# Threshold attention with a feed-forward on one core: inverted sums sent through DRAM, values a step later, and other orders of the steps

## The chip, the cores and the metric

The kernel runs on one core of a Trainium2 chip. The core has TensorE (matrix products into PSUM), VectorE, ScalarE and GpSimd for elementwise work, SyncE (SP) that only starts transfers here, and 16 DMA engines that carry what SP, ScalarE and GpSimd start. The metric is the device time of one execution in microseconds; the kernel before has a median of 528.99 us over three runs (527.98 to 530.42).

## The reference

Attention over 8 batches, 8 heads, 576 positions and 64 features, which keeps only scores close to their row's maximum, and then two dense layers over the 4608 x 512 result:

```python
scores = scale * np.matmul(q, k.transpose(0, 1, 3, 2))
thresh = np.max(scores, axis=-1, keepdims=True) - tau
scores = np.where(scores >= thresh, scores, -1000000000.0)
attn = np.exp(scores - np.max(scores, axis=-1, keepdims=True))
attn = attn / (np.sum(attn, axis=-1, keepdims=True) + 1e-09)
x = np.matmul(attn, v)             # then (batch, position, head and feature)
h = x @ w_in                       # 512 -> 2048
out = np.maximum(0.01 * h, h) @ w_out   # 2048 -> 512
```

## The kernel before

**Tiles.** Two heads make a pair; there are 32 pairs, and two pairs make a *couple*, so 16 couples, two to a batch. The 1152 query rows of a couple and head slot are cut into nine *steps* of 128 rows: steps 0 to 3 belong to the first pair, 4 to 7 to the second, step 8 takes the last 64 rows of both. In each step the two heads of the pair are worked one beside the other ("first" and "second").

**One step.** `s_mm` (L146) makes the scores of both heads from queries and keys split into a high and a low float16 part (three products). VectorE's `s_max` instruction (L182) scales them, writes them to `sn` and gives the negated row maximum; GpSimd makes a threshold `nth` from it (L187). Then a head goes one of two ways. Either ScalarE takes one exponential (L192), and a step later VectorE masks it and adds up the row (L215, in `s_mask`); or the head is *direct*: ScalarE makes two passes (L198, L202), the second of which gives the row's sum, and VectorE does nothing more. The weights `W` of both heads are turned by a DMA transpose that SP starts (L221) into `wT`.

**A couple's sums and values.** After the ninth mask the 18 sums of each of 128 partitions are inverted: `sums_0` adds a small number on GpSimd, `sums_1` inverts on VectorE and makes the high float16 part on GpSimd, `sums_2` makes the low part on VectorE. `sums_3` turns both parts by one product (L247) and ScalarE takes the result to `row`. `sums_4` spreads the rows over 64 partitions each by five or six products with a selecting matrix (L264); ScalarE takes the result to `rc` (L269). `values` (L272) multiplies `wT` by V on TensorE (20 products), and VectorE multiplies by `rc` on its way to `xT` (L290). In PSUM, the turns of queries and keys (`prep`, L123), the turned sums, the spread and the values all use the one pair of banks "A"; scores have two pairs and the dense layers two single banks "u".

**The dense layers.** When a batch's values are there (couple 2, 4, ..., step 6), `push_main` and `push_tail` put its work on a list of *units*: four products of 512 columns each into a bank "u" (L302, then ScalarE's L306), or four products of the second layer (L317). The units are handed out over the following 18 steps, in shares set by the tuple `share`; `ahead_of` says how many of a step's units come before its second head.

**The order.** All instructions are in program order on their engines; the loop at the end writes that order. For each step it takes a string of parts ("scores", "values", "first", "units", "turn_qk", "spread", "evict", "second", "more", "mask", "soon") and calls them in turn. "evict" and "soon" run ScalarE's and VectorE's deferred evictions. The couple's values come in steps 3 and 5 of the next couple, after the spreads in steps 2 and 4. Loads of q and k and the outputs go over SP's queue, V and the dense weights over GpSimd's.

Of the kernel before, what the change touches and what calls it, by code (L numbers as in the profile page):

```python
# [9 lines left out]
FP32 = mybir.dt.float32  # L10
# [6 lines left out]
def kernel(  # L17
# [24 lines left out]
    sb = ctx.enter_context(tc.tile_pool(name="sb", bufs=1))  # L42
    ps = ctx.enter_context(tc.tile_pool(name="ps", bufs=1, space=bass.MemoryType.PSUM))
# [68 lines left out]
    due = []  # L112

# [9 lines left out]
    def prep(p, i, tag="A", bufs=1):  # L123


        t = nat[p]
        pt = pair_of_banks(tag, bufs).rearrange("p a b -> p (a b)")
        for c in range(4 + i):

            nc.tensor.matmul(  # L130
                out=pt[0:128, ds(c * 128, 128)],
                lhsT=t[0:128, 4 * i + c, :, :].rearrange("p h d -> p (h d)"),
                rhs=I32[:, :],
                is_transpose=True, skip_group_check=True,
            )
# [3 lines left out]
        due.append(lambda: nc.scalar.activation(out=hi[:, :], in_=pt[:, 0:N], func=AF.Copy, bias=0.0, scale=QS))  # L139
        soon.append(lambda: nc.vector.scalar_tensor_tensor(  # L140
            out=lo[:, :], in0=pt[:, 0:N], scalar=QS, in1=hi[:, :],
            op0=OP.mult, op1=OP.subtract,
        ))
        qk.setdefault(p, {})[i] = (hi, lo)

    def s_mm(c, t):  # L146


        out = [ps.tile([128, 2, 512], FP32, tag="s", bufs=2, name="s") for _ in range(2)]
        if t < 8:  # L150
            srcs = [(2 * c + t // 4, 0, ds(t % 4 * 128, 128), ds(0, 128))]
        else:
            srcs = [(2 * c + e, 1, ds(576, 64), ds(64 * e, 64)) for e in range(2)]
        for half in range(2):
            for ti, (a, b) in enumerate(((0, 0), (1, 0), (0, 1))):
                for p, i, cols, po in srcs:
                    for h in range(2):
                        r = ds(h * 64, 64)
                        nc.tensor.matmul(  # L159
                            out=out[h][po, half, 0:288], lhsT=qk[p][i][a][r, cols],  # L160
                            rhs=qk[p][1][b][r, ds(half * 288, 288)],
                            start=(ti == 0), stop=(ti == 2), skip_group_check=True,
                        )
        sc[(c, t)] = out

    live, dens = {}, {}

    def s_max(c, t, h, direct):
# [3 lines left out]
        if t == 0 and h == 0:  # L172
            dens[c] = sb.tile([128, 18], FP32, tag="den", bufs=2, name="den")
        if h == 0:
# [20 lines left out]
        else:  # L195
# [8 lines left out]
                accum_out=dens[c][:, 2 * t + h:2 * t + h + 1],  # L204
            )

    def s_mask(c, t):
# [5 lines left out]
        for h in range(2):  # L213
            if h not in masked:
# [3 lines left out]
                    accum_out=dens[c][:, 2 * t + h:2 * t + h + 1],  # L218
                )
        q0 = 512 if t == 8 else t * 128 + (t // 4) * 128  # L220
# [4 lines left out]
    def sums_0(c):  # L225

# [6 lines left out]
    def sums_1(c):  # L233
        d1, rr = inv[c]
        nc.vector.reciprocal(out=rr[:, :], in_=d1[:, :])
        nc.gpsimd.tensor_scalar(out=r2[:, 0, 0:18], in0=rr[:, :], scalar1=1.0 / RS, scalar2=0.0,
                                op0=OP.mult, op1=OP.add)

    def sums_2(c):
        d1, rr = inv[c]  # L240
        nc.vector.scalar_tensor_tensor(out=r2[:, 1, 0:18], in0=rr[:, :], scalar=1.0 / RS, in1=r2[:, 0, 0:18],
                                       op0=OP.mult, op1=OP.subtract)

    def sums_3(c):

# [6 lines left out]

    def sums_4(c, e):

        row = rows[c]
# [12 lines left out]
        rc = sb.tile([128, 576], FP32, tag="rc", bufs=2, name="rc")  # L268
        due.append(lambda: nc.scalar.activation(out=rc[:, :], in_=t[:, 0:576], func=AF.Copy, bias=0.0, scale=1.0))  # L269
        rcs[e] = rc  # L270

    def values(c, e):  # L272
# [12 lines left out]
        rc = rcs.pop(e)  # L285
# [3 lines left out]
        def mul():  # L289
            nc.vector.tensor_tensor(  # L290
# [45 lines left out]
    def push_main(b):  # L336

# [42 lines left out]
    with tc.manual_schedule():  # L380
# [15 lines left out]
        for p in range(1, 3):  # L396
# [12 lines left out]
        before = "scores turn_qk evict first second mask soon"  # L409
        orders = {  # L410
            0: "scores turn_qk evict units first second more mask soon",
            1: "scores invert first units rest more second mask soon",
            3: "scores values first units second more mask soon",
            5: "scores first values units second more mask soon",
            6: "scores first turn_qk evict units more second mask soon",
            8: "scores first units turn_qk evict more second mask soon",
        }
        credit = 0.0
        w_at = [1 + i for i in range(32)]
        prev = None  # L420
        for c in range(NC + 1):
            last = c == NC
            for t in range(NT):
                step = c * NT + t
                if c > 1 and c % 2 == 0 and t == 6:

                    if c % 4 == 2 and c > 2:
                        push_tail(c // 2 - 3, 1)
# [5 lines left out]
                nxt = {6: (2 * c + 2, 0), 7: (2 * c + 2, 1), 8: (2 * c + 3, 0), 0: (2 * c + 1, 1)}  # L434
                if c == 0:
                    nxt[0], nxt[1] = (1, 0), (1, 1)
                pi = nxt.get(t)
                if pi is not None and pi[0] >= NP:
                    pi = None

                ahead = [share[i % NT] for i in range(step, (c // 2 * 2 + (0 if c % 2 == 0 and t < 6 else 2)) * NT + 6)]
                credit = min(credit, 1.0) + (len(units) - credit) * share[t] / sum(ahead)
                n = min(int(credit + 0.01), len(units))
                credit -= n
                n1 = min(n, (n + ahead_of[t]) // 2)
                direct = tau_f <= 16.0 and (
                    t not in (0, 1, 3) if c < 3 else t in (2, 5, 7, 8) or not any(u[0] for u in units[:n]))
                direct0 = tau_f <= 16.0 and c < 3 and t in (0, 3, 5)

                if c == 0 and t < 2 or c < 2 and t == 6:  # L450
                    order = before
                else:
                    order = orders.get(t, plain)
                    if c == 1 and t == 0:
                        order = "scores first turn_qk evict second mask soon"
                for part in order.split():
                    if part == "scores" and not last:
                        s_mm(c, t)
                    elif part == "values" and c > 0:
                        values(c - 1, t // 2 - 1)  # L460
                    elif part == "first" and not last:
                        s_max(c, t, 0, direct0)
                    elif part == "second" and not last:
                        s_max(c, t, 1, direct)
                    elif part == "invert" and c > 0:
                        sums_1(c - 1)
                    elif part == "rest" and c > 0:
                        sums_2(c - 1)
                    elif part == "units":
                        work(n1)  # L470
                    elif part == "more":
                        if c > 0 and t == 1:
                            work(n - n1 - 1)
                            sums_3(c - 1)
                            work(1 if n > n1 else 0)
                        else:
                            work(n - n1)
                    elif part == "turn_qk" and pi is not None:
                        prep(*pi)
                    elif part == "spread" and c > 0 and t in (2, 4):  # L480
                        sums_4(c - 1, t // 2 - 1)
                    elif part == "evict":
                        run(take(due))
                    elif part == "mask":
                        if prev is not None:
                            s_mask(*prev)
                        prev = None if last else (c, t)
                    elif part == "soon":
                        run(take(soon))
                if c > 0 and t == 0:  # L490
                    sums_0(c - 1)
                if c == 0 and 0 < t < 6:
                    load_v(0, t - 1)
                if c % 2 == 0 and c > 0 and t >= 4 and c // 2 < B:
                    load_v(c // 2, t - 4)
                for i in range(32):
                    if w_at[i] == step:
                        load_w(i)
                if t < 4 and 2 * c + 3 < NP:
                    load_qk(2 * c + 3, t // 2, t % 2)  # L500
                elif 4 <= t < 8 and 2 * c + 4 < NP:
                    load_qk(2 * c + 4, t // 2 - 2, t % 2)
# [36 lines left out]
```

## Time and profile before

| | |
|---|---|
| Runs (us) | 528.99, 530.42, 527.98 |
| Profiled execution | 528.58 us, its span 526.8 us |
| TensorE, VectorE, ScalarE, GpSimd busy | 94%, 79%, 84%, 35% |
| Mean granted TensorE clock | 0.969 |
| DMA | 80.5 MB, mean 153 GB/s |
| Chain that ended last | TensorE 83%, ScalarE 7%, VectorE 5% |

How to read it: busy time is what an engine's instructions took, matmuls overlap, and their ends are modelled. "[1.06 <-ACT hi L139]" behind a line says that the engine stood idle for 1.06 us before it and that ScalarE's instruction of line 139 ended the wait. PEclk is the granted clock in tenths. In the table of stretches the figure in brackets is the number of instructions. A DMA's landing is the time from its issue to its completion.

### The profile page before, as it was taken

How to read it: one execution, taken by the hardware profiler on the slowest of the kernel's cores; microseconds unless marked ns; L12 is line 12 of the kernel's file. 1: busy time of each engine (PE TensorE's matmuls, PEld its weight loads, DVE VectorE, ACT ScalarE, POOL GpSimd, SP SyncE). 2: the span in 40 equal slices, each digit the busy share in tenths (PEclk: the TensorE clock that was granted, in tenths of full speed). 3: DMA queues.
4: the chain of work that ended last, by engine and by line, in shares of the span. 5: the costliest groups of instructions: out<-in, count | busy, mean ns of one | idle time of the engine just before them, and what ended most of it. 6: DMA issues, size and time to landing. Idle time of an engine off the chain costs nothing.

```text
span 526.8 us, 12333 instructions
## 1 busy us (share of the span) xinstructions
PE 494.7 (94%) x4384; PEld 272.9 (52%) x4384; DVE 414.7 (79%) x1076; ACT 444.0 (84%) x795; POOL 186.4 (35%) x430
## 2 busy tenths in 40 slices
PE   5577787999999999999999999999999999999996
PEld 3344444555555566555555566555555565545444
DVE  5878887998899888998899888998899888982000
ACT  3896979989999899989898999989898999983622
POOL 0754446543443234323443234323433244321000
PEclk9786969999999999999999999999999999999999
DMA  6999999998997899887999689887998799853011
GB/s 154 137 164 184 205 186 198 206 183 175 164 186 145 152 173 168 167 142 165 183 170 142 150 176 188 146 138 156 189 164 152 147 169 154 116 85 93 40 41 60
DMA packets 266813, 80.50 MB, mean 153 GB/s; under 512 B 251904, under 2 KB 264192, under 8 KB 266752
## 3 DMA queue, kind: packets, MB, share of 16 engines
q1 hardware_dynamic: 249136, 70.68, 75.0%
q0 software_dynamic: 17536, 8.92, 14.8%
q8 instruction: 34, 0.56, 0.5%
q14 instruction: 27, 0.22, 0.1%
q10 hardware_dynamic: 80, 0.13, 0.1%
HBM read 36.70 MB, written 9.44 MB: 88 GB/s over the span
## 4 chain that ended last, share of the span: by engine, by line
PE 83%; ACT 7%; DVE 5%; issue 2%; DMA 2%; POOL 0%; SPq 0%; DVEq 0%; ACTq 0%; POOLq 0%
PE u L317 24%; PE u L302 22%; PE s L159 21%; PE A L280 8%; PE A L130 6%; DVE sn L182 3%; ACT W L202 2%; ACT far L198 2%; ACT e L192 2%; PE A L264 1%; DMA nat<-in_q_dram 1%; DVE W L215 1%; DMA nat<-in_k_dram 1%; ACT hi L139 1%; ACT gM L306 0%
## 5 line engine op out<-in xcount | busy, mean ns | idle before, releaser
L182 DVE TENSOR_SCALAR_CACHE_REDUCE sn<-s 128x576 f32<-128x576 f32 x288 | 207.6, 754 | 41.9 <-PE s L159 40.2
L187 POOL TENSOR_SCALAR nth<-nmx 128x1 f32<-128x1 f32 x288 | 125.6, 436 | 242.2 <-DVE sn L182 219.1
L192 ACT ACTIVATE e<-sn,nmx 128x576 f16<-128x576 f32 x181 | 137.6, 770 | 17.6 <-DVE sn L182 16.4
L215 DVE SCALAR_TENSOR_TENSOR W<-sn,nth,e 128x576 f16<-128x576 f32 x181 | 144.3, 814 | 0.0
L302 PE MATMUL u<-xT,win 128*128 128x512 f16 x512 | 122.7, 380 | 0.4 <-ACT gM L306 0.4
L317 PE MATMUL u<-wout,gM 128*128 128x512 f16 x512 | 122.1, 380 | 0.0
L159 PEld LDWEIGHTS <-hi 64*128 64x128 f16 (+1 forms) x1280 | 65.9, 99 | 70.4 <-issue 53.4
L159 PE MATMUL s<-hi,hi 64*128 64x288 f16 x512 | 87.6, 300 | 11.4 <-DVE sn L182 9.7
L159 PE MATMUL s<-hi,lo 64*128 64x288 f16 (+1 forms) x640 | 93.1, 294 | 0.0
L159 PE MATMUL s<-lo,hi 64*128 64x288 f16 (+1 forms) x640 | 92.8, 293 | 0.0
L198 ACT ACTIVATE far<-sn,nth 128x576 f32<-128x576 f32 x107 | 82.5, 771 | 8.2 <-POOL nth L187 6.3
L302 PEld LDWEIGHTS <-win 128*128 128x128 f16 x768 | 61.2, 98 | 52.5 <-issue 8.4
L202 ACT ACTIVATE W<-far,ntau 128x576 f16<-128x576 f32 x107 | 83.0, 775 | 3.5
L306 ACT ACTIVATE gM<-u 128x512 f16<-128x512 f32 x128 | 71.5, 590 | 6.8 <-PE u L302 6.8
L317 PEld LDWEIGHTS <-gM 128*128 128x128 f16 x512 | 46.5, 98 | 52.6 <-issue 7.9
L140 DVE SCALAR_TENSOR_TENSOR lo<-A,hi 128x512 f16<-128x512 f32 (+1 forms) x63 | 47.6, 755 | 17.0 <-ACT hi L139 16.6
L130 PE MATMUL A<-I,nat 128*128 128x128 f32 x283 | 45.9, 291 | 10.4 <-DVE lo L140 5.1
L139 ACT ACTIVATE hi<-A 128x512 f16<-128x512 f32 (+1 forms) x63 | 40.0, 636 | 10.1 <-PE A L130 10.1
L280 PE MATMUL A<-wT,V 128*64 128x288 f16 x640 | 48.0, 298 | 0.0
L130 PEld LDWEIGHTS A<-I,nat 128*128 128x128 f32 x283 | 32.1, 145 | 26.0 <-DVE lo L140 13.8
L280 PEld LDWEIGHTS <-V 128*64 128x64 f16 x640 | 35.1, 113 | 11.7 <-issue 8.0
L328 ACT ACTIVATE osb<-u 128x512 f32<-128x512 f32 x35 | 20.6, 590 | 23.7 <-PE u L317 23.7
(44 smaller groups left out, 302.8 us busy)
## 6 DMA issues: line engine op xcount, KB each, us to landing
nat<-in_q_dram SPq DMA_DIRECT2D x32, 256.0 KB, 3.6
nat<-in_k_dram SPq DMA_DIRECT2D x32, 256.0 KB, 3.8
out_dram<-osb SPq DMA_DIRECT2D x16, 512.0 KB, 3.6
wT<-W SPq DMA_TRANSPOSE x144, 4.1
V<-in_v_dram POOLq DMA_DIRECT2D x8, 256.0 KB, 5.7
win<-in_moe_w_in_dram POOLq DMA_DIRECT2D x16, 128.0 KB, 5.2
V<-in_v_dram POOLq DMA_DIRECT2D x16, 128.0 KB, 4.9
wout<-in_moe_w_out_dram POOLq DMA_DIRECT2D x16, 128.0 KB, 4.7
```

The source lines that it names most:

```text
L130: nc.tensor.matmul(out=pt[0:128, ds(c * 128, 128)], lhsT=t[0:128, 4 * i + c, :, :].rearrange("p h d -> p (h d)"), rhs=I32[:, :], is_transp ...
L159: nc.tensor.matmul(out=out[h][po, half, 0:288], lhsT=qk[p][i][a][r, cols], rhs=qk[p][1][b][r, ds(half * 288, 288)], start=(ti == 0), stop= ...
L182: nc.vector.tensor_scalar(out=sn[:, h, :].rearrange("p (a b) -> p a b", a=2), in0=s_[:, :, 0:288], scalar1=-BS, scalar2=None, op0=OP.mult, ...
L187: nc.gpsimd.tensor_scalar(out=nth[:, h:h + 1], in0=nmx[:, h:h + 1], scalar1=1.0, scalar2=tau_f, op0=OP.mult, op1=OP.add,)
L192: nc.scalar.activation(out=e[:, h, :], in_=sn[:, h, :], func=AF.Exp, bias=nmx[:, h:h + 1], scale=-1.0,)
L198: nc.scalar.activation(out=far[:, :], in_=sn[:, h, :], func=AF.Prelu, bias=nth[:, h:h + 1], scale=-1.0, alpha=BIG,)
L202: nc.scalar.activation(out=w[:, ds(h * 576, 576)], in_=far[:, :], func=AF.Exp, bias=ntau[:, 0:1], scale=1.0, accum_out=dens[c][:, 2 * t + ...
L215: nc.vector.scalar_tensor_tensor(out=w[:, ds(h * 576, 576)], in0=sn[:, h, :], scalar=nth[:, h:h + 1], in1=e[:, h, :], op0=OP.is_le, op1=OP ...
L280: nc.tensor.matmul(out=t[ds(h * 64, 64), half, 0:288], lhsT=vb[:, g, h, kb, :], rhs=wT[:, 4 * h + kb, ds(e * 576 + half * 288, 288)], star ...
L302: nc.tensor.matmul(out=t[:, ts(j, N)], lhsT=w_in16[:, gi, ts(j0 + j, 128)], rhs=xs[gi], start=(gi == 0), stop=(gi == NG - 1), skip_group_c ...
L306: nc.scalar.activation(out=g_out, in_=t[:, 0:nj * N].rearrange("p (j n) -> p j n", j=nj), func=AF.Prelu, bias=0.0, scale=1.0, alpha=0.01)
L317: nc.tensor.matmul(out=t[:, :], lhsT=g_in(j), rhs=w_out16[:, j, :], start=(j == 0), stop=(j == NJ - 1), skip_group_check=True,)
```

## The change

For couples 3 to 14 (`by_dma`) the sums' spread no longer uses products. The inverted sums are turned in float32 by one product of 18 columns of weights, ScalarE takes the 18 x 128 result to `row32`, GpSimd stores it to a scratch tensor in DRAM (`sums_d`, in step 1) and reads it back with four loads that each repeat one row of 640 numbers over 64 partitions (`sums_b`, in step 2). The columns of the sums are laid out so that a row of the turned sums is one head's rows in order. Couples 0 to 2 and 15 keep the old way.

The first values of a couple come in step 4 instead of 3 from couple 3 on; the second stay in step 5, in some couples behind units. The strings of parts are written anew in single letters for five classes of couples (0, 1, 2, odd and even from 3 on). The sets of direct heads are given by class (`d0` for the first head, `d1` for the second, with `d1n` for those which are never made direct for lack of first-layer units); over the whole kernel 116 heads are direct instead of 107 (8, 7, 8 instead of 9, 9, 9 in couples 0 to 2). `share` has 18 entries, `up` takes the place of `ahead_of`. Loads are placed by a table, at the same steps as before.

```diff
+def by_dma(c):
+    return 3 <= c < 15
+
+def col(c, t, h):
+    if not by_dma(c):
+        return 2 * t + h
+    return 9 * h + (t if t < 4 else 4 if t == 8 else t + 1)
...
-                accum_out=dens[c][:, 2 * t + h:2 * t + h + 1],
+                accum_out=dens[c][:, col(c, t, h):col(c, t, h) + 1],
...
 def sums_1(c):
     nc.vector.reciprocal(out=rr[:, :], in_=d1[:, :])
+    if by_dma(c):
+        return
...
 def sums_3(c):
+    if by_dma(c):
+        d1, rr = inv[c]
+        t = pair_of_banks().rearrange("p a b -> p (a b)")
+        nc.tensor.matmul(out=t[0:18, 0:128], lhsT=rr[:, :], rhs=I32[:, :], is_transpose=True,
+                         skip_group_check=True)
+        row = sb.tile([18, 128], FP32, tag="row32", bufs=2, name="row32")
+        due.append(lambda: (nc.scalar.activation(out=row[:, :], in_=t[0:18, 0:128], func=AF.Copy, bias=0.0, scale=1.0), was.add(("row", c))))
+        rows[c] = row
+        return
...
+def sums_d(c):
+    d = dr.tile([18, 128], FP32, tag="dr", bufs=2, name="dr")
+    nc.gpsimd.dma_start(out=d[:, :], in_=rows[c][:, :])
+    rows[c] = d
+
+def sums_b(c):
+    d = rows[c]
+    for e in range(2):
+        rc = sb.tile([128, 640], FP32, tag="rc", bufs=2, name="rc")
+        src = d.rearrange("(h i) q -> h (i q)", h=2)[:, ds(512 * e, 640)]
+        for h in range(2):
+            nc.gpsimd.dma_start(out=rc[ds(64 * h, 64), :], in_=src[h:h + 1, :].to_broadcast([64, 640]))
+        rcs[e] = rc[:, ds(64 * e, 576)]
...
-share = (20, 21, 23, 13, 20, 13, 26, 29, 26)
-ahead_of = (3, 3, 1, 3, -1, 1, 1, 1, -1)
-plain = "scores first units turn_qk evict spread evict second more mask soon"
+share = (23, 21, 23, 16, 20, 13, 26, 29, 32, 23, 27, 23, 16, 20, 10, 29, 29, 32)
+d0 = [[0, 1, 3, 5], [0, 3, 5], [0, 2, 3], [], []]
+d1 = [[3, 4, 5, 7], [3, 6, 7, 8], [3, 4, 5, 7, 8], [2, 3, 4, 6, 8], [0, 2, 3, 4, 5, 8]]
+d1n = [[0, 6], [3], [3], [0, 2, 3], [2, 3, 4]]
```

The order of the parts for odd couples from 3 on, one string for each step (S scores, 0 and 1 the heads, P a turn of q or k, h evictions, U, u and w units, r inversion, T turn of the sums, D store, R loads, Q old spread, V values, M masks, L deferred work of VectorE, d the sums' first instruction):

```
'S Pd h U w 0 h 1 u M d L', 'r S U 0 x T u h D 1 w M L', 'S w 0 U Q0 h 1 u R M L',
'S 0 u U w 1 M L', 'S V0 0 w U Q1 h 1 u M L', 'S U 0 V1 1 u M L', ...
```

More of the change, by code (lines that the diff above doesn't have):

```diff
@@ L225, in sums_0 @@
     def sums_0(c):
+        assert ("mask", c, 8) in was
+        was.add(("d", c))
         d1 = sb.tile([128, 18], FP32, tag="d1", bufs=1, name="d1")
@@ L336, in push_main @@
     def push_main(b):
+        assert all(("x", b, g) in was for g in range(NG))
         xs = [xTs[(b, g)][:, ds(g % 2 * 64, 512)] for g in range(NG)]
@@ L404 @@
         run(take(soon))
-        share = (20, 21, 23, 13, 20, 13, 26, 29, 26)
-        ahead_of = (3, 3, 1, 3, -1, 1, 1, 1, -1)
-        plain = "scores first units turn_qk evict spread evict second more mask soon"
[L409 to L417, printed above, removed]
@@ new lines, with at @@
+        credit = 0.0
+        plan = {}
+        def at(step, f):
+            plan.setdefault(step, []).append(f)
+        for b in range(B):
+            for i, x in enumerate([[1, 2, 3, 4, 5], [22, 23, 24, 25, 26]][b] if b < 2 else range(18 * b + 4, 18 * b + 9)):
+                at(x, lambda b=b, i=i: load_v(b, i))
+        for i, x in enumerate([1, 2, 3, 4, 5, 6, 7, 8, 9, 10, 11, 12, 13, 14, 15, 16, 17, 18, 19, 20, 21, 22, 23, 24, 25, 26, 27, 28, 29, 30, 31, 32]):
+            at(x, lambda i=i: load_w(i))
@@ L420 @@
+        for p in range(3, NP):
+            for x in range(4):
+                at((p - 3) // 2 * 9 + (p - 3) % 2 * 4 + x + 0, lambda p=p, x=x: load_qk(p, x // 2, x % 2))
+        for x in sorted(s_ for s_ in plan if s_ < 0):
+            for f in plan[x]:
+                f()
         prev = None
@@ L433 @@
                         push_tail(c // 2 - 2, 1)
[L434 to L455, printed above, removed]
@@ L456, with target @@
-                for part in order.split():
-                    if part == "scores" and not last:
-                        s_mm(c, t)
[L459 to L463, printed above, removed]
+                def target(x):
+                    return x * NT + (6 if x == 2 else 6)
+                nx = c // 2 * 2
@@ new lines, with count @@
+                if step >= target(nx) or c < 2 and 0:
+                    nx += 2
+                def count():
+                    global_ = sum(share[i % 18] for i in range(step, max(target(nx), step + 1)))
+                    return (len(units) - credit) * share[ph] / global_
+                n = None
+                for o in orders[cl][t].split():
+                    if o == "G":
+                        if c > 1 and c % 2 == 0:
+                            push()
+                            nx = c // 2 * 2 + 2
+                        continue
+                    if n is None:
+                        credit = min(credit, 1.0) + count()
+                        n = min(int(credit + 0.01), len(units))
+                        credit -= n
+                        k1 = min(n, max(0, (n + up[cl][t]) // 2))
+                        heads = [u[0] for u in units[:n]]
+                    if o == "S" and not last:
+                        s_mm(c, t)
+                    elif o[0] == "V" and c > 0:
+                        values(c - 1, int(o[1]))
+                    elif o == "0" and not last:
+                        s_max(c, t, 0, tau_f <= 16.0 and (t in d0[cl]))
+                    elif o == "1" and not last:
+                        direct = tau_f <= 16.0 and (t in d1[cl] or c > 2 and t not in d1n[cl] and not any(heads))
@@ L483 @@
                         run(take(due))
-                    elif part == "mask":
+                    elif o[0] == "Q" and c > 0 and not by_dma(c - 1):
+                        sums_4(c - 1, int(o[1]))
+                    elif o == "M":
                         if prev is not None:
                             s_mask(*prev)
-                        prev = None if last else (c, t)
-                    elif part == "soon":
+                            prev = None
+                        if not last:
+                            prev = (c, t)
+                    elif o == "L":
@@ L489 @@
                         run(take(soon))
[L490 to L502, printed above, removed]
+                for f in plan.get(step, ()):
+                    f()
```

91 lines of the change are left out of this document (63 added, 28 removed).

## The prediction

> **What bounds the kernel now.** I read the share of each engine in 40 slices first, then the same by stretches of time, then TensorE's timeline over one couple in the middle.
>
> ```profile
> PE   5577787999999999999999999999999999999996
> DVE  5878887998899888998899888998899888982000
> ACT  3896979989999899989898999989898999983622
> ...
> PEclk9786969999999999999999999999999999999999
> ```
>
> ```profile
> core 0: us, PE busy (x) PEld busy (x) DVE busy (x) ACT busy (x) POOL busy (x), PEclk, DMA share, GB/s
> ...
> 26.00:40.00 14.00, 9.79 (x89) 5.91 (x85) 10.84 (x28) 13.61 (x26) 7.35 (x16) 0.86 1.42 165
> ...
> 53.00:66.00 13.00, 9.11 (x97) 5.90 (x97) 11.10 (x27) 12.60 (x23) 6.11 (x14) 0.92 1.17 205
> ...
> 79.00:92.00 13.00, 10.35 (x109) 6.34 (x108) 9.57 (x24) 12.69 (x24) 8.11 (x17) 1.00 1.29 199
> ...
> 316.00:369.00 53.00, 53.00 (x488) 29.35 (x487) 47.59 (x126) 48.99 (x89) 18.39 (x43) 1.00 0.95 157
> ```
>
> Two regimes. From about 92 us to the end TensorE is never idle (53.00 of 53 us), ScalarE is at 92% and VectorE at 90%: there a microsecond of TensorE work is a microsecond of time. Before 92 us there are no units yet; TensorE idles 27 us, and where two keys and queries are turned (the three stretches above) ScalarE is full, at 97%. The timeline of all engines shows what that costs: VectorE stands still until ScalarE, behind its double passes, has evicted `hi`.
>
> ```profile
> 58.27 0.69 DVE L140 SCALAR_TENSOR_TENSOR lo<-A,hi 128x512 f16<-128x512 f32 x1 [1.06 <-ACT hi L139]
> ...
> 86.37 0.69 DVE L140 SCALAR_TENSOR_TENSOR lo<-A,hi 128x512 f16<-128x512 f32 x1 [1.80 <-ACT hi L139]
> ```
>
> **Term 1: the spread's products go (12 couples).** TensorE's timeline in couple 8, start and length:
>
> ```profile
> 245.50 0.22 PE L247 MATMUL A<-I,r 128*128 128x128 f16 x1
> 245.65 0.30 PE L159 MATMUL s<-hi,hi 64*128 64x288 f16 x2
> ...
> 247.37 0.42 PE L264 MATMUL A<-row,sel 128*128 128x128 f16 x5
> 247.62 1.03 PE L317 MATMUL u<-wout,gM 128*128 128x512 f16 x4
> ...
> 252.58 0.43 PE L264 MATMUL A<-row,sel 128*128 128x64 f16 x6
> 252.84 1.89 PE L317 MATMUL u<-wout,gM 128*128 128x512 f16 x8
> ```
>
> What counts is from one start to the next: 0.25 us for the first five, 0.26 us for the six, so 0.51 us a couple. All twelve couples lie in the full regime: 12 x 0.51 = 6.1 us off the path. The turn of the sums (L247, 0.15 us start to start) is replaced by a turn in float32. The rows have float32 turns of 128 columns (L130), four of them in 0.50 us at 237.34, so 0.12 us each; the mean duration of one, if nothing overlapped, is 0.29. Bounds: -0.4 to +1.7 us over twelve; I take 0, since in this regime they overlap. ScalarE loses two evictions of 0.63 us a couple and keeps a row of about 0.28; VectorE loses 0.17 and GpSimd 0.22: none is on the path there, so 0.
>
> **Term 2: the way of the sums through DRAM.** New, per couple, on GpSimd: one store of 9 KB and four loads of 164 KB. The transfers issued by GpSimd after 100 us are the nearest rows:
>
> ```profile
> V<-in_v_dram POOLq DMA_DIRECT2D x12, 128.0 KB, 4.4
> ...
> V<-in_v_dram POOLq DMA_DIRECT2D x12, 32.0 KB, 3.4
> ```
>
> Call the store's landing d and a load's b. I lay the changed order over the measured lengths (scores 0.84 us, a unit of four products 0.87, values 1.35), with zero at the start of step 1 of a couple. Scores, two units, the turn: 2.73. ScalarE's row is out at about 3.5; the store is issued there, lands at 3.5 + d. GpSimd then stands in front of the first load until d is over, and issues a load each 0.65 us (issues of V last 0.64 to 0.92). Both loads of the first half land at 4.15 + d + b. Step 4 begins at 7.87; VectorE reaches the product with the sums 3.04 us later (248.58 to 251.62 in the old couple), at 10.9. If the sums are late VectorE waits, which is free until the second values need the pair of banks: they are due at 12.6, so the product must start by 11.8. The margin is d + b = 7.65 us (in couple 4, whose step 3 has one unit, 7.2). The rows: 3.4 + 4.4 = 7.8, a stall of about 0.15 us a couple. The lowest landings of V in this regime (2.8 and 2.8) give none; 4.1 (a store of 128 KB) and 6.0 (the slowest V) give 2.5 us a couple, 29 us in all. The loads here have 64 rows in one piece each, V four pieces a row with a change of type, so I put b a little under its row; with scatter I charge 1.5 us in all.
>
> The Trainium skill, DMA: Bandwidth & Descriptors, section "Anatomy of one DMA", gives about 2.0 us plus bytes over 436 GB/s for a transfer that GpSimd issues; an estimate by it is 2.0 + 2.4 = 4.4 us for d + b, no stall, and a sum 1.5 us lower. The 32 KB of V that take 3.4 us under this kernel's traffic stand against the page, so the sum goes by the rows.
>
> What is queued behind: on GpSimd the thresholds (L187) of step 1's second head wait for the store, those of step 3 for the four loads, until about 3.5 + 3.4 + 4 x 0.65 = 9.5. ScalarE's direct pass of step 3 needs them and starts near 10 instead of 8.2 to 9.5. ScalarE has the slack to take this back in steps 4 and 5, but in couples 4, 8 and 12 it is still about 1 us late at the evictions of step 6, where the next unit then waits up to 0.5 us: I charge 0.7 us in all, bounds 0 and 6 (0.5 in each couple). The traffic grows by 0.66 MB per 29 us, 22 GB/s on 157; stretches before 92 us ran at 205, and TensorE waited for `wT` 1.3 us in the whole run, so 0. SP's queue keeps its order.
>
> **Term 3: other heads go direct.** A direct head costs ScalarE two passes, start to start 1.56 us against 0.69, and spares VectorE a mask of 0.81 (0.88 with its read). Couples 0 to 2 have 8, 7, 8 instead of 9 each. In the full stretches, two direct heads fewer each stand ahead of the late `hi`: 1.74 us less on ScalarE, 1.6 more on VectorE. At 79 to 92 VectorE has room (9.57 + 1.6 of 11.3): about 1.5 us won of the wait of 1.80. At 26 to 40 and 53 to 66 VectorE becomes equally full: about 1.0 and 0.7. Sum 3.2; I take 2.7 since masks also come into the loop between scores and minima. Bounds: 5.2 won (3 x 1.74) to 3.5 lost (four masks all exposed). In couples 3 to 15, 13 more heads are direct: 13 x 0.87 = 11 us on ScalarE against 12 x 2 x 0.63 = 15 taken away, so it stays below TensorE; VectorE loses 13 x 0.88. Cost 0 while TensorE covers it.
>
> **Moved steps.** Values and their product come a step later: nobody waits for them before the units of the next pair. At the very end eight products of old outputs (1.7 us) stand between the last values and the first new unit before, four (0.87) after; VectorE's product of 0.75 us just fits into them. The shares move units between steps, not their number. 0.
>
> **Sum.** The profiled execution took 528.58 us, 1.8 more than its span of 526.8, and 0.4 less than the median 528.99. 528.58 - 6.1 - 2.7 + 1.5 + 0.7 = 522.0; I give 522.0 for the median too.
>
> **Rivals.**
> A: the sums are late for good. Speaks for it: rows at 7.8 against a margin of 7.65, and V landings up to 6.0. Against: the waits of V and the weights in the full regime are nowhere in the list of waits. Each us over the margin costs 12. At d + b = 9.2, 1.55 us over: 528.58 - 8.8 + 18.6 + 0.7 = 539. It decides at 8.3 (no gain left); slower by 0.5% from 8.5. The Trainium skill, SBUF — State Buffer, box "The DVE blocks DMA trap (SWDGE)", would feed it: GpSimd's descriptors wait while VectorE holds the shared port. The rows bear out a hold for thresholds (0.70 us beside a mask, 0.19 alone), but issues of V never stretched past 0.92.
> B: the start doesn't move, VectorE taking ScalarE's place as its bound: 528.58 - 6.1 + 2.2 = 524.7. For it: two stretches come out equally full.
> C: ScalarE takes over in the full regime, since the waits on thresholds fall on an engine at 92%: term 2's 6 us and the start's 2.7 leave 528.58 - 6.1 - 2.7 + 1.5 + 6 = 527.3.
> D: nothing is late: 522.0 - 2.2, and the start's whole 5.2: 517.3.
>
> **How the numbers follow.** Forecast (520 to 524) 0.33; B 0.16; D 0.15; C 0.13; A 0.23. The range from 517 to 532 leaves out the far half of A and a third of D, 0.16 together. About 0.5% (2.6 us) is what a measurement of this kernel tells from no change. Faster by more: forecast, B, D and a few of C, 0.66. Same: most of C and the near part of A, 0.15. Slower: the rest of A, 0.19.
>
> **What would show it.** Right: TensorE full from about 89 us on, two couples in 58.0 us instead of 59.0 (178.98 to 238.00 in the chain), hardly any wait of VectorE's product on the loads, store and four loads landing within 7.7 us in sum of d and b, `lo` waiting less for `hi` before 92 us. Wrong: TensorE waiting for VectorE's product at the second values once a couple; units waiting for ScalarE's `gM`; or VectorE full at the start with the same 92 us.

## The result, and the profile after

The changed kernel takes 535.3 us (median of 6 runs, 531.91 to 537.37), the kernel before 528.14 us beside it: a ratio of 1.0115 (95%: 1.009 to 1.0139; the ratio is taken over the runs and is not the quotient of the two medians). It is slower, and outside the predicted range of 517 to 532. The profiled execution took 536.01 us with a span of 534.2, against 528.58 and 526.8 before: 7.4 us more span.

The busy share in 40 slices, from the page of the changed kernel:

```profile
PE   5677779999799999989899999999999999999996
...
DVE  5888989988698887978598888888898868972000
ACT  3886889988799989988699889988899988984622
...
PEclk9776879999999999999899999999999999999999
```

TensorE's row of 9s, unbroken before from the eighth slice on, now has gaps in slices 11, 18 and 20. In the last of them (254 to 267 us) VectorE falls to 5, ScalarE to 6 and the granted clock to 8 tenths. The same by stretches of time, first the changed kernel and then the one before (columns as before):

```profile
core 0: us, PE busy (x) PEld busy (x) DVE busy (x) ACT busy (x) POOL busy (x), PEclk, DMA share, GB/s
...
26.00:40.00 14.00, 10.44 (x87) 6.11 (x82) 12.01 (x32) 11.90 (x21) 6.87 (x16) 0.74 1.38 215
53.00:66.00 13.00, 9.13 (x96) 5.93 (x93) 12.53 (x33) 10.97 (x19) 6.06 (x13) 0.91 1.25 182
79.00:92.00 13.00, 11.57 (x116) 6.93 (x115) 11.58 (x30) 12.41 (x23) 8.60 (x19) 1.00 1.23 157
211.00:264.00 53.00, 48.80 (x414) 25.93 (x412) 41.28 (x109) 44.38 (x82) 19.30 (x48) 0.98 0.94 172
316.00:369.00 53.00, 52.09 (x506) 29.87 (x504) 44.74 (x115) 49.87 (x91) 21.28 (x51) 1.00 1.06 180
```

```profile
211.00:264.00 53.00, 53.00 (x468) 28.23 (x467) 47.08 (x123) 48.38 (x88) 18.33 (x44) 1.00 0.88 164
```

From 211 to 264 us TensorE, full before, is now busy for 48.80 of 53 us. What it waits for stands in the list of TensorE's waits of the changed kernel (line and what it waited for: us in total, times, longest):

```profile
PE A L336 <- DVE xT L349: 7.7, 5, 2.5
...
PE A L132 <- DVE xT L349: 3.7, 4, 1.3
```

The values (L336) and the turns of q and k (L132) wait for VectorE's product `xT`; two of the four turns (1.8 us) lie ahead of couple 3. In the kernel before no values wait for it, and two turns ahead of couple 3 do, for 1.0 us. VectorE's own list says why the product is late:

```profile
DVE xT L349 <- DMA rc<-dr: 19.9, 14, 3.6
DVE lo L144 <- ACT hi L141: 11.6, 16, 1.9
```

The product stands 14 times, 19.9 us in all, before loads of the sums. (The second line is for later: VectorE's wait for `hi` was 17.6 us before.) The chain of the changed kernel from 249 to 266 us shows the worst case, couple 8 (start, length, what):

```profile
248.58 0.58 ACT osb L387
249.16 0.16 ACT row L279
249.32 0.28 issue
249.60 3.88 DMA dr<-row
253.48 0.28 issue
253.76 0.44 POOL rc L304
254.20 0.13 issue
254.33 6.56 DMA rc<-dr
...
261.01 0.77 DVE xT L349
261.78 0.04 issue
261.82 2.61 PE A L336 x20
```

No engine bounds this stretch: the chain runs from ScalarE's row through the store (3.88 us), GpSimd's second load (6.56 us) and the product to the second values. Over the whole run the transfers carry 16% of the chain and TensorE 54%, where TensorE carried 83% before.

Lengths of couples, from one first minimum (L199, L182 before) to the next, give the account. A couple is named here by its own steps; the sums and values that are worked in them are those of the couple before it, so the way through DRAM is walked in couples 4 to 15.

| | before | after | difference |
|---|---|---|---|
| couples 0 to 2 (start of couple 3) | 94.78 | 93.40 | -1.38 |
| couple 3 | 28.22 | 29.44 | +1.22 |
| couples 4 to 14 | 324.07 | 332.27 | +8.20 |
| couple 15 to the end of the span | 79.7 | 79.1 | -0.6 |

Couple 3 has one unit of 0.87 us more, which is missing at the end; most of these two differences is that shift. In couples 4 to 14 TensorE was never idle; now it is idle for 11.0 us, of which 9.65 are waits for a late `xT` (7.77 at the second values, 1.88 at turns behind it in couples 4 and 7). Where nothing is late, odd couples take 28.98 us instead of 29.46, and even ones from 6 on 29.46 or 29.47 instead of 29.49 to 29.56: the two together 58.45 (couples 9 and 10), where 58.0 was forecast and 59.0 was the time before.

### The profile page after: what moved, and what is told of

Same layout as the page of the kernel before. It is cut to its first block, busy times and chain, and to the rows that moved or that the text cites. A ratio compares the mean times of both kernels' runs of the same rounds, so it can differ in the third digit from the quotient of the medians.

```text
span 534.2 us, 12130 instructions
## 1 busy us (share of the span) xinstructions
PE 492.0 (92%) x4252; PEld 269.7 (50%) x4252; DVE 405.8 (76%) x1046; ACT 439.5 (82%) x789; POOL 202.1 (38%) x478
## 4 chain that ended last, share of the span: by engine, by line
PE 54%; DMA 16%; ACT 14%; DVE 7%; issue 5%; POOL 2%; DVEq 0%; SPq 0%; POOLq 0%; ACTq 0%
PE u L376 18%; PE u L361 13%; PE s L165 12%; DMA rc<-dr 9%; PE A L336 5%; ACT e L209 5%; DMA dr<-row 5%; PE A L132 5%; DVE sn L199 4%; ACT gM L365 3%; ACT far L215 2%; ACT W L219 2%; DVE W L232 2%; DVE xT L349 1%; POOL rc L304 1%
## 5 line engine op out<-in xcount | busy, mean ns | idle before, releaser
L199 DVE TENSOR_SCALAR_CACHE_REDUCE sn<-s 128x576 f32<-128x576 f32 x288 | 206.5, 754 | 41.9 <-PE s L165 41.1
L204 POOL TENSOR_SCALAR nth<-nmx 128x1 f32<-128x1 f32 x288 | 111.3, 387 | 191.7 <-DVE sn L199 177.0
L209 ACT ACTIVATE e<-sn,nmx 128x576 f16<-128x576 f32 x172 | 129.5, 766 | 20.0 <-DVE sn L199 19.2
L232 DVE SCALAR_TENSOR_TENSOR W<-sn,nth,e 128x576 f16<-128x576 f32 x172 | 137.7, 815 | 0.6 <-POOL nth L204 0.6
L215 ACT ACTIVATE far<-sn,nth 128x576 f32<-128x576 f32 x116 | 89.3, 770 | 22.7 <-POOL nth L204 21.9
L219 ACT ACTIVATE W<-far,ntau 128x576 f16<-128x576 f32 x116 | 89.9, 775 | 3.8
L365 ACT ACTIVATE gM<-u 128x512 f16<-128x512 f32 x128 | 73.0, 589 | 7.1 <-PE u L361 5.9
L132 PE MATMUL A<-I,nat 128*128 128x128 f32 x283 | 45.9, 292 | 11.8 <-DMA nat<-in_q_dram 4.5
L336 PE MATMUL A<-wT,V 128*64 128x288 f16 x640 | 48.9, 303 | 8.3 <-DVE xT L349 7.7
L349 DVE TENSOR_TENSOR xT<-A,rc 128x576 f16<-128x576 f32 x32 | 24.2, 756 | 31.7 <-DMA rc<-dr 19.9
L336 PEld LDWEIGHTS <-V 128*64 128x64 f16 x640 | 37.6, 115 | 18.7 <-issue 15.9
L132 PEld LDWEIGHTS A<-I,nat 128*128 128x128 f32 x283 | 32.9, 146 | 26.9 <-DVE lo L144 8.7
```

Source lines behind the costliest of these rows:

```text
L132: nc.tensor.matmul(out=pt[0:128, ds(c * 128, 128)], lhsT=t[0:128, 4 * i + c, :, :].rearrange("p h d -> p (h d)"), rhs=I32[:, :], is_transp ...
L199: nc.vector.tensor_scalar(out=sn[:, h, :].rearrange("p (a b) -> p a b", a=2), in0=s_[:, :, 0:288], scalar1=-BS, scalar2=None, op0=OP.mult, ...
L204: nc.gpsimd.tensor_scalar(out=nth[:, h:h + 1], in0=nmx[:, h:h + 1], scalar1=1.0, scalar2=tau_f, op0=OP.mult, op1=OP.add,)
L209: nc.scalar.activation(out=e[:, h, :], in_=sn[:, h, :], func=AF.Exp, bias=nmx[:, h:h + 1], scale=-1.0,)
L215: nc.scalar.activation(out=far[:, :], in_=sn[:, h, :], func=AF.Prelu, bias=nth[:, h:h + 1], scale=-1.0, alpha=BIG,)
L219: nc.scalar.activation(out=w[:, ds(h * 576, 576)], in_=far[:, :], func=AF.Exp, bias=ntau[:, 0:1], scale=1.0, accum_out=dens[c][:, col(c, t ...
```

## The experiments

The theory after the result was rival A: the sums come too late. Against it stood that GpSimd, standing before its transfers, delays thresholds and so ScalarE (rival C), that the additional traffic as such does it, or that the new orders are worse by themselves.

### 1. The loads don't wait for the store (e2_free_loads)

```diff
-        src = d.rearrange("(h i) q -> h (i q)", h=2)[:, ds(512 * e, 640)]
+        src = q[c // 2, 0:2, ds(8 * e, 10), :].rearrange("h a d -> h (a d)")
```

> The changed kernel with its store, but the four loads read a piece of q instead of what was stored, so they need not wait for the store (the scaling by the sums is wrong; all work and traffic stay). The loads start about 3 us earlier. Late sums as the cause: the waits for the product go, 524 to 526. Traffic or the new orders as the cause: 533 or more. GpSimd's blocked thresholds as the cause: between, about 530, since the four issues still stand in front of them.

525.52 us, 0.9934 of before (0.991 to 0.9958), span 522.9. TensorE's waits:

```profile
PE A L336 <- ACT rc L325: 0.3, 1, 0.3
PE A L336 <- DVE xT L349: 0.2, 1, 0.2
```

The same transfers of the same size (landing 5.0 us as before) cost nothing once they aren't chained: traffic as such is out. GpSimd doesn't stand in front of the loads here either, so the run has fewer blocked thresholds as well as earlier sums, but not many fewer: GpSimd stands as long as in the changed kernel in front of the store (20.6 us, until ScalarE's row is out), and ScalarE still waits 18.0 us for thresholds, against 21.9 in the changed kernel and 6.3 before. TensorE is full all the same. The run also shows what the change is worth with nothing late: 3.9 us of span.

### 2. Half the bytes (e8_half_rows)

```diff
-            row = sb.tile([18, 128], FP32, tag="row32", bufs=2, name="row32")
+            row = sb.tile([18, 128], FP16, tag="row32", bufs=2, name="row32")
```

and the same for `dr` and `rc`.

> The changed kernel with the turned sums, the scratch tensor and the spread rows in float16: the same transfers at half the bytes (80 KB a load). If the loads' 5 us are the time of their bytes among the other traffic, they fall to 4 us or less and the waits for the product to half: 529 to 531. If they are latency, or the waits behind other queues: 534 to 536.

526.18 us, 0.9956 (0.9941 to 0.9971): better than expected. The transfers issued after 100 us, of the changed kernel and then of this one:

```profile
rc<-dr POOLq DMA_DIRECT2D x48, 160.0 KB, 5.0
...
nat<-in_k_dram SPq DMA_DIRECT2D x23, 256.0 KB, 5.9
...
dr<-row POOLq DMA_DIRECT2D x12, 9.0 KB, 2.6
```

```profile
nat<-in_k_dram SPq DMA_DIRECT2D x23, 256.0 KB, 5.0
...
rc<-dr POOLq DMA_DIRECT2D x48, 80.0 KB, 4.1
...
dr<-row POOLq DMA_DIRECT2D x12, 4.5 KB, 2.6
```

Loads land 0.9 us sooner, and so do the loads of k. In the list of all waits GpSimd stands nearly as long in front of the loads (11.3 us instead of 13.1) and thresholds are nearly as late (ScalarE waits 19.5 us for them instead of 21.9), yet TensorE is full but for 1.8 us:

```profile
ACT far L215 <- POOL nth L204: 19.5, 29, 1.3
POOL rc L304 <- DMA dr<-row: 11.3, 12, 2.5
...
PE A L336 <- DVE xT L349: 1.8, 2, 1.5
```

```profile
211.00:264.00 53.00, 52.75 (x456) 27.76 (x451) 45.42 (x117) 47.98 (x88) 21.20 (x52) 1.00 0.90 165
```

So it was the late sums, not the thresholds. Couple by couple the law is plain. Store to both loads of the first half landed ("way"), and TensorE's wait at the second values, us:

| couple | 4 | 5 | 6 | 7 | 8 | 9 | 10 | 11 | 12 | 13 | 14 | 15 |
|---|---|---|---|---|---|---|---|---|---|---|---|---|
| way, changed kernel | 10.10 | 7.93 | 8.28 | 8.98 | 11.29 | 7.92 | 8.66 | 8.83 | 8.81 | 8.15 | 10.23 | 8.14 |
| wait | 2.08 | 0 | 0 | 0.94 | 2.50 | 0 | 0 | 0.79 | 0 | 0.11 | 1.35 | 0 |
| way, half the bytes | 9.54 | 6.93 | 8.09 | 6.98 | 9.03 | 7.28 | 7.58 | 7.64 | 8.00 | 7.92 | 8.84 | 7.29 |
| wait | 1.52 | 0 | 0 | 0 | 0.25 | 0 | 0 | 0 | 0 | 0 | 0 | 0 |

Up to couple 14 the wait is the way less a limit: 8.02 in couple 4, 8.04 in odd couples, 8.8 to 8.9 in even ones, the same in both kernels.

### 3. The row earlier (e4_early_row)

```diff
-'S r 0 U x T u h D 1 w M L'
+'S r x T h 0 D U u 1 w M L'
```

for step 1 of even couples, and alike for odd ones (whose string in the changed kernel is `r S 0 U x T u h D 1 w M L`, with the first head ahead of the units): turn and row come behind the scores, the store ahead of the units.

> The changed kernel, but for couples from 2 on the turn of the sums and ScalarE's row come right behind the scores of step 1 and the store before the units. The store leaves about 2 us earlier, the loads 1 to 2 us. Late sums as the cause: TensorE's wait of 9.5 us falls to about 4, 529 to 531. Traffic or orders as the cause: unchanged at 533 to 536.

530.25 us, 1.0019 (0.9999 to 1.0038): 5 us under the changed kernel, as late sums demand. The store leaves 2.4 to 2.5 us after the start of step 1 (3.4 in couple 4, where the turn has to wait) instead of 3.4 to 4.1. Left are 0.94 and 1.44 in couple 4 and 0.64 in couple 6; the turn of the sums now waits for VectorE's inversion instead, in couples 3 and 4 and after the last (here the waits of couple 4):

```profile
127.33 0.27 PE L276 MATMUL A<-I,rr 128*18 128x128 f32 x1 [0.85 <-DVE rr L257]
...
140.22 1.42 PE L336 MATMUL A<-wT,V 128*64 128x288 f16 x20 [0.94 <-DVE xT L349]
144.88 0.66 PE L132 MATMUL A<-I,nat 128*128 128x128 f32 x4 [1.44 <-DVE xT L349]
```

### 4. Both (e9_half_early)

The edits of 2 and 3 together (the early row from couple 4 on).

> The changed kernel with float16 rows, and in couples 4 to 15 the turn and ScalarE's row right behind the scores of step 1. With half the bytes one wait of TensorE for VectorE's product of 1.5 us is left, in couple 4. Late sums as the cause: it goes, 524 to 525.5, faster than the kernel before by 0.6 to 0.9%. If it goes but the turn then waits for the inverted sums in each couple: 526 or more.

526.02 us against 529.25, 0.9939 (0.9921 to 0.9957): faster than both kernels, but not the expected 524 to 525.5 and no clear step beyond half the bytes alone. Of the waits 0.69 us in couple 4 is left, but the turn waits 0.85 there, and every couple is 0.07 us longer (29.05 and 29.53), since the turn now stands alone between scores and units.

### 5. The products back, in the new orders (e1_products)

```diff
-        return 3 <= c < 15
+        return False
...
-'S 0 u U w 1 M L', 'S V0 0 w U Q1 h 1 u M L'
+'S V0 0 u U w 1 M L', 'S 0 w U Q1 h 1 u M L'
```

and alike for even couples.

> The changed kernel, but all couples spread their sums by products, with first values in step 3 again; orders, shares and direct heads stay new. If the late sums are the cause (TensorE waits 9.5 us in all for VectorE's product in the changed kernel's trace), this ends those waits and gives up the products' 6 us: about 528 to 530. If the new orders, shares and direct heads are the cause, it stays at 533 or more.

538.55 us, 1.0174 (1.015 to 1.0198). Not the clean control it was meant to be. The new orders put the spread behind both units of a step, and the values then wait for ScalarE to empty the banks:

```profile
PE A L336 <- ACT rc L325: 7.5, 17, 0.7
```

These orders don't suit the products. That says nothing on the changed kernel's own stall, but the orders can't be judged apart from the way through DRAM. Experiment 1 has what both bring together when nothing is late: 3.9 us less span than before.

### 6. The same with unused transfers (e5_spare_dma)

```diff
+            r32 = sb.tile([18, 128], FP32, tag="row32", bufs=2, name="row32")
+            due.append(lambda: nc.scalar.activation(out=r32[:, :], in_=t[0:18, 0:128], func=AF.Copy, bias=0.0, scale=1.0))
...
+            rc = sb.tile([128, 592], FP32, tag="rcs", bufs=2, name="rcs")
...
+                nc.gpsimd.dma_start(out=rc[ds(64 * h, 64), :], in_=src[h:h + 1, :].to_broadcast([64, 592]))
```

on top of 5: store and loads run, nobody reads them.

> As the run with products everywhere, and on top of it a row, the store and four loads at their places in couples 3 to 14 (592 columns a row instead of 640), which nobody uses. Late sums as the cause: no more than 1.5 us over the run with products. GpSimd's blocked thresholds or the traffic as the cause: 5 us or more over it.

545.93 us, 1.0314 (1.0289 to 1.0339), 7.4 more than 5, against at most 1.5 if late sums were all there is: a miss. Here ScalarE's waits for thresholds grow from 6.6 to 14.5 us, and as it also evicts `rc`, the values wait longer for it:

```profile
PE A L339 <- ACT rc L328: 12.5, 21, 1.6
...
PE A L339 <- DMA wT<-W: 1.2, 3, 0.8
```

Blocked thresholds, rival C's mechanism, are the likely cause where TensorE waits for ScalarE, but this run doesn't separate them from the twelve rows that ScalarE takes besides, nor from the traffic, which shows in the 1.2 us that the values now wait for `wT`. In the changed kernel no `rc` comes from ScalarE in these couples, and experiments 1 and 2 show late thresholds harmless there.

### 7. The first three couples alone (e3_start)

```diff
-                    t not in (0, 1, 3) if c < 3 else t in (2, 5, 7, 8) or not any(u[0] for u in units[:n]))
-                direct0 = tau_f <= 16.0 and c < 3 and t in (0, 3, 5)
+                    t in ((3, 4, 5, 7), (3, 6, 7, 8), (3, 4, 5, 7, 8))[c] if c < 3 else t in (2, 5, 7, 8) or not any(u[0] for u in units[:n]))
+                direct0 = tau_f <= 16.0 and c < 3 and t in ((0, 1, 3, 5), (0, 3, 5), (0, 2, 3))[c]
```

in the kernel before.

> The kernel before, with the changed kernel's sets of direct heads in couples 0 to 2 and nothing else. The changed kernel reaches couple 3 earlier by 1.4 us in its trace. If the sets did that and it lasts: 526.5 to 527. If it is given back once TensorE is full, or the prediction's 2.7 us was right: 528 or 525.5.

528.35 against 528.68 us, 1.0007 (0.9973 to 1.0042): not the expected 526.5 to 527, and with runs from 526.43 to 534.21 too coarse for 1.5 us. One trace of each kernel shows it: span 525.3 instead of 526.8, couple 3 starts at 93.26 instead of 94.78, and the 1.5 us stay won to the end (couple 15 at 445.57 instead of 447.08). The times don't confirm it.

### 8. The way through DRAM in the old orders (e6_dma_old_orders, e7_dma_early_start, e12_half_old_orders)

The kernel before with the way through DRAM for couples 3 to 14 and, there only, new strings:

```diff
+                if by_dma(c - 1):
+                    order = {
+                        1: "scores invert first units turn_sums more store second mask soon",
+                        2: "scores first units second more load mask soon",
+                        3: plain,
+                        4: "scores values first units second more mask soon",
+                    }.get(t, order)
```

> The kernel before with its own orders, shares and direct heads, and the way through DRAM for couples 3 to 14 at the changed kernel's places (turn behind the units of step 1, store, loads in step 2, values in steps 4 and 5). Late sums as the cause: the same waits of TensorE for VectorE's product, some 10 us, against 5.6 us of products that go: 531 to 535. If the new orders alone made the changed kernel slower: 522 to 524.

547.93 us, 1.0386 (1.0329 to 1.0442). Worse than expected: `xT` is late in ten couples, and each couple loses another 0.4 us or more, because step 3 has only one unit left and the scores of step 4 wait for VectorE:

```profile
PE A L315 <- DVE xT L325: 13.2, 10, 3.1
PE s L160 <- DVE sn L191: 12.7, 31, 1.3
```

```profile
226.55 0.28 PE L160 MATMUL s<-hi,hi 64*128 64x288 f16 x1
227.23 0.28 PE L160 MATMUL s<-hi,hi 64*128 64x288 f16 x1 [0.40 <-DVE sn L191]
```

The next one adds the early row and the direct heads of couples 0 to 2:

```diff
-                        1: "scores invert first units turn_sums more store second mask soon",
+                        1: "scores invert turn_sums first store units second more mask soon",
```

> As the run with the way through DRAM in the old orders, but the turn and the row come right behind the scores of step 1 and the store behind the first head, and couples 0 to 2 have the changed kernel's direct heads. Late sums as the cause: the store leaves about 2 us earlier, TensorE's waits fall to about 3 us: 523 to 526, faster than the kernel before. If the length of the loads is what decides and not their start: 529 or more.

534.2 us, 1.0116 (1.0071 to 1.016). 14 us better, of which 2.3 us are won ahead of couple 3, but not at the expected 523 to 526: the short step 3 stays (its scores take 1.50 us instead of 0.84, the unit before 1.08), and a couple without late sums takes 29.7 to 29.9 us, more than before. The third tries to mend that, with half the bytes and the shares of steps 3 and 4 exchanged:

```diff
-        share = (20, 21, 23, 13, 20, 13, 26, 29, 26)
+        share = (20, 21, 23, 20, 13, 13, 26, 29, 26)
```

> The old orders with the way through DRAM, early row and new direct heads at the start, with float16 rows, and the shares of steps 3 and 4 exchanged, since the values moved from step 3 to 4. In the run without this exchange step 3 had one unit only, and TensorE waited for VectorE in every couple (29.9 us a couple instead of 29.5). If that was the reason: 29.1 us a couple, 523 to 525. If the old orders have another loss: 529 or more.

535.65 us, 1.0151 (1.0106 to 1.0195), a miss again. The waits only change place: units of step 3 wait for ScalarE's `gM` (5.1 us in 6 waits), and the second values, now with a unit fewer ahead of them, for the product (5.8 us in 10). In the old orders, then, moving the values a step back cost more than the products save, in three tries; the new strings and shares make the move without this loss (experiment 1).

### 9. Fewer split units (e10_half_grouped)

```diff
-[3, 3, 1, 0, 1, 0, -1, 1, -1]]
+[3, 3, 1, 0, 1, 3, -1, 1, -1]]
```

(the last row of `up`, even couples, step 5) on experiment 4, with couple 2 by DRAM too.

> As the run before it, and the units of step 5 in even couples stand together ahead of the second values (a unit that stands alone costs 0.1 us more), and couple 2 goes the way through DRAM too (0.45 us). If these prices from the trace are right: 0.7 to 1.2 us under the run before it; if the second values are then late for the next pair's units: over it.

528.42 us, 0.9976 (0.9959 to 0.9993): 2.4 us over experiment 4 instead of 0.7 to 1.2 under it. Its profiled execution was the shortest of twelve (526.38 us, a span of 524.6 as in experiment 4), so the trace doesn't show what makes the others longer. In it, with the units ahead of the second values a unit waits 0.53 us for ScalarE's `osb` in couple 10.

### 10. No output stores beside it (e11_no_stores)

```diff
+                if b < 6:
+                    return
```

in front of the output's store.

> The changed kernel without the large output stores of batches 0 to 5 (12 stores of 512 KB; that part of the output is left out). If these stores are what makes the loads of some couples slow (the slowest, couple 8, has one in flight): the waits for the product in couples 4 and 8 go, 529 to 531. If it is the queries' and keys' loads and the transposes: 533 to 536.

529.2 us, 1.0002 (0.9973 to 1.0031), 6 us under the changed kernel; runs spread from 527.26 to 534.14. Its profiled execution was one of the longer (532.04): from couple 4 on `xT` is still late by 3.5 us at the values, in four couples, and by 2.6 at turns, but in couple 8 by 0.60 (at a turn) instead of 2.50. The median way is 8.36 us instead of 8.73, couple 8's 8.45 instead of 11.29; couple 11's grew from 8.83 to 9.56. So the 512 KB stores seem to be part of what stretches the way, and not all of it; what else does stays open.

## Why the prediction was wrong

Two steps failed. The larger is the size of term 2, the wait for sums that come through DRAM: 1.5 us charged, 9.65 measured, and 1.5 more behind the longest wait. The smaller is term 1, where 6.1 us were to be won and 3.3 were. The start gave 1.3 us less than forecast.

**Products gone (term 1).** The spread did leave: 5.68 us in couples 4 to 14. The step that failed is that all of it is won: "all twelve couples lie in the full regime: 12 x 0.51 = 6.1 us off the path". Odd couples won 0.48, even ones from 6 on 0.03 to 0.09, couple 4 0.69 where nothing was late (experiment 1). Comparing couple 8 with the late sums away (experiment 1) with before: products -0.51, first-layer units +0.37, second-layer units +0.12, turn of the sums +0.06, scores and turns of q and k -0.11; sum -0.07. The first-layer part lies at a single unit, for which TensorE stands idle for 0.2 us until ScalarE's `gM` is done; it starts 1.23 us after the unit ahead of it instead of 0.87. The second-layer part is the cutting into groups: the last unit of a group takes 0.96 us start to start where scores or values follow, against 0.87 in a row, and the new shares make six such ends of this couple's second-layer units where there were five. I had costed the new shares at nothing ("the shares move units between steps, not their number"). The float32 turn costs 0.20 instead of 0.15 start to start, inside its bounds.

**Way through DRAM (term 2).** The mechanism, its place and its sign of trouble were as I had put them, "TensorE waiting for VectorE's product at the second values once a couple"; in five couples of twelve it happened (and by 0.11 us in a sixth). The size failed: 1.5 us were charged and 9.65 came. Three parts:

- The limit. I had 8.30 us from store to landing (7.65 and an issue of 0.65); it is 8.8 in even couples but 8.04 in odd ones, where the store leaves at 4.09 instead of 3.5, and 8.02 in couple 4 (4.04).
- The transfers. By the rows 7.8 + 0.65 = 8.45; the median is 8.73 (store 2.63, second load 4.91, between them GpSimd's own issues). The rows were good to 0.3 us at the median.
- The spread. At a constant 8.45 the measured limits would give 5 x 0.41 + 0.43 = 2.5 us, at a constant 8.73 some 4.2, and the real ways from 7.92 to 11.29 give 7.77. Turns held up behind the late product add 1.9.

The last is the step: where the mean lies on the limit, the late half of the ways is paid and the early half pays nothing back, and I charged only what the mean gives. The rows had the scatter: the 32 KB of V landed in 2.81 to 5.08 us after 100 us, the larger pieces in 3.57 to 6.73. (The 6.0 that I gave as the slowest V is not the slowest.) The bound I had set for the highest rows, 29 us, was as wrong on the other side. The estimate by the Trainium skill, DMA: Bandwidth & Descriptors, section "Anatomy of one DMA", 4.4 us for store and load together, is not borne out under this traffic: 2.6 and 4.9 at the median, 3.9 and 6.6 in couple 8.

**Thresholds.** 0.7 us charged; ScalarE did wait 21.9 us for them, and TensorE lost nothing by it that a trace shows. Units do wait for `gM` in couples 4, 8 and 12, where I had put this cost, 0.2 us each; but they wait as long in experiment 5, which has no transfer of sums and where ScalarE waits 6.6 us for thresholds. So these waits come with the new orders, shares and direct heads. That late thresholds are harmless rests on experiments 1 and 2; experiment 6 has an order in which they may cost.

**Start (term 3).** 2.7 us forecast, 1.4 measured (1.5 alone, in the trace of experiment 7). VectorE's wait for `hi` fell from 17.6 to 11.6 us as meant, but the first two stretches gave 0.2 and 0.0 us instead of 1.0 and 0.7, the last 1.2 instead of 1.5. In the second VectorE became the bound (12.53 of 13 us busy, 11.10 before), which is rival B's mechanism. In the first neither VectorE nor ScalarE is full (12.01 and 11.90 of 14 us), and the granted clock was lower in this execution, 0.74 instead of 0.86; what held this stretch stays open.

**Rivals.** A came in part, at 535.3 instead of 539: not late for good with a way 1.4 us over the rows, but late in five couples of twelve with a median 0.3 over them. GpSimd's issues of the store and the loads lasted 0.52 to 0.59 us throughout, so no hold of the issues fed it. The span with measured terms: 526.8 - 1.4 (start) - 3.3 (couples 4 to 14 with nothing late, experiment 1) + 9.65 (waits for `xT`) + 1.5 (couple 8 behind its wait, below) + 0.6 (the shifted unit and the end) = 533.9, against 534.2 measured.

## What to carry to other kernels

A round trip through DRAM must be budgeted by its slowest landings, not by its median, wherever a buffer of the busiest engine waits behind it; one couple that is late by 2 us eats what four of the odd couples save. If such a way is at its limit, halve its bytes or start it sooner before anything else: here the one was worth about 8 us and the other 5. Work taken off a full engine is won only as far as the order around it is fitted again: here 3.3 of 5.7 us.

## What was not expected of the hardware

- Loads issued one after another land later and later. The four loads of a couple, issued 0.51 to 0.59 us apart, took 4.0, 4.9, 5.3 and 5.7 us at the median (2.99 the fastest first, 8.51 the slowest fourth). The Trainium skill, SBUF — State Buffer, section "Can I just issue two DMAs to hit both halves?", says that two transfers to the lower and the upper half of the partitions nearly serialize; these loads go to such halves, and the trace agrees in direction.
- More traffic showed in the landing of others far more than in the mean rate: the 256 KB loads of k after 100 us went from 3.6 to 5.9 us while the mean rate of the run rose from 153 to 166 GB/s, and back to 5.0 with half the bytes of the sums. Why these and not the loads of q (3.6 and 3.8), the runs don't show.
- After TensorE's wait of 2.50 us in couple 8 the 20 products of the values took 2.54 us instead of 1.35 and the unit behind them 1.26 instead of 0.97: 1.5 us on top of the wait. The granted clock was 0.50 from 261.6 to 265.0 us, and 1.00 before and after. The length of a wait alone doesn't decide this: waits of 2.08 and 1.35 us cost no more than themselves, and after one of 3.13 us in the first kernel of experiment 8 (at 172.5 us) the clock stayed at 1.00 and the values took 1.35 us.
